# An attention and two matrix stages on one core: from slot 16 on three engines issue in a written order, with the second attention in smaller steps

## The chip, the core and the metric

The kernel runs on one core of a Trainium2 chip. PE multiplies matrices into PSUM (eight banks), ACT does functions and copies, DVE elementwise work and transposes, POOL further elementwise work, and SP issues DMAs. Each engine takes its own instructions in order and waits on semaphores for the others. The metric is the device time of one execution in microseconds. Before the change it is 1663.2 us, the median of three runs (1661.97 to 1664.64).

## The reference

```python
# q, k, v: 8 batches x 8 heads x 576 x 64; p: 8 x 8 x 32 x 64; all float32
p_packed = sm_attn(p, k, v)                    # 32 packed rows per head
out = sm_attn(q, p_packed, p_packed)           # second attention, 576 rows
x = out as tokens x 512                        # 4608 tokens
h = x @ moe_w_in; g = h * cos(h); x = g @ moe_w_out          # 512 -> 2048 -> 512
h = x @ moe2_w_in                                            # 512 -> 2048
P = a0 + a1*h + a2*h**2 + a3*h**3
Q = 1 + |b0|*|h| + |b1|*h**2
out = (P / (Q + 1e-6)) @ moe2_w_out
```

## The kernel before

The program has three parts. The first, up to some 120 us, makes the packed rows of every batch. The second part, which the change touches, has 128 slots, 16 for each of the 8 batches. It doesn't form the attention's output: the second attention gives only its weights (ah and al, a value and its rest, which together stand for one float32), and the packed rows are multiplied into w_in beforehand (W', tile wq, high and low part). The third part is the last matrix stage (L773 and L860).

A slot n covers 288 tokens (half a batch) and 256 of the 2048 hidden columns. `mm_h` has 12 matmuls of 288 columns (L580) that give h in PSUM. `chain1` makes g from it: u on ACT (L605), r on DVE (L606), the absolute value and the sine on ACT (L610, L611), g on DVE (L612). One slot later `finish_g` splits g into gh (ACT, L66) and gl (DVE, L67). `mm_y(n-2)` takes gh and gl two slots later: 24 matmuls (L634) that add to four PSUM banks y0 to y3. After the eight slots of a half each bank is copied as yh and yl (L66, L67) and stored (L656, L657). For batch 0 the half is done in two pieces, and a piece stored earlier, yp, is added first (L652).

h has two PSUM buffers, used in turn. The scores of the second attention (L192) take the next buffer of the same two. So the h that follows scores gets the buffer of the h just ahead of them, which is free once g has read it.

Beside this, while batch b runs, the following is done on ACT, DVE and POOL. `attn2_steps` is a generator that does the second attention of batch b+1 in steps: transposes of q (qT) and packed rows (ppb), scores and the maximum (sT), Exp on ACT (L376, with a table load ahead, and another one back to the sine), the sums (sm), scaling and transposing (aT), ah and al. `split_wq` splits a quarter of W' for the next batch: the high part on ACT (L66), the rest on DVE (L67); quarter j serves slots 2j, 2j+1, 2j+8 and 2j+9 of its batch. `conv_w2` turns every third slot a piece of the third part's weights into two words: cvf on DVE and POOL (L79, L84, L88), cvh on ACT (L92), cvl on POOL (L93), two stores.

The order of instructions on each engine is not that of the code. A scheduler chooses it at build time from the dependences and the free buffers, and `hold` only keeps an instruction behind another one. The order within PE's stream is therefore a mixture: pieces of y and of h of several slots alternate.

Of the kernel before, what the change touches and what calls it, by code (L numbers as in the profile page):

```python
# [20 lines left out]
def pack_attention_moe_moe_kernel(  # L21
# [90 lines left out]
    if True:  # L112
# [210 lines left out]
        def attn2_steps(b, pool, new_ps, tg, now):  # L323
            def load(g):
                t = pool.tile([128, C, D], F32, tag="qx", bufs=1, name="qx")
                nc.sync.dma_start(out=t, in_=q[b, 4 * g:4 * g + 4].rearrange("h (j c) d -> (h j) c d", c=C))
                return t

            def tile(shape, dt, nm):
                tag, bufs = tg.get(nm, (nm, 1))  # L330
                return pool.tile(shape, dt, tag=tag, bufs=bufs, name=nm)

            t = load(0)
            if b == 1:
                ppb_t[0] = pool.tile([128, NDB, 4, M], F32, name="ppb")
                nc.gpsimd.memset(ppb_t[0], 0.0)
            ppb = ppb_t[0]
            sT = pool.tile([128, G, C, M], F32, tag="sT", bufs=1, name="sT")
            yield
            for g in range(G):  # L340
                qT = tile([128, NDB, C, 32], F32, "qT")
                hold(
                    nc.vector.transpose(  # L343
                        out=qT.rearrange("p e c j -> p c e j"), in_=t.rearrange("p c (e i) -> p c e i", e=NDB)
                    ),
                    now(),
                )
                if b == 0:
                    ppT = tile([128, NDB, M], F32, "ppT")
                    hold(nc.vector.transpose(out=ppT.rearrange("p e m -> p (e m)"), in_=pp[:, b * G + g]), now())  # L350
                else:
                    ppT = ppb
                    for h in range(4):
                        r = slice(32 * h, 32 * h + 32)
                        hold(
                            nc.vector.transpose(
                                out=ppT[r, :, h], in_=pp[r, b * G + g].rearrange("p (e i) -> p e i", e=NDB)
                            ),
                            now(),
                        )  # L360
# [14 lines left out]
                yield  # L375
            nc.scalar.activation(out=sT, in_=sT, func=AF.Exp, scale=scale)  # L376
            sm = pool.tile([128, G, C], F32, tag="sm2", bufs=1, name="sm2")
            nc.vector.tensor_reduce(out=sm, in_=sT, op=ALU.add, axis=AX.X)
            nc.vector.tensor_scalar(out=sm, in0=sm, scalar1=1e-9, scalar2=None, op0=ALU.add)
            nc.vector.reciprocal(out=sm, in_=sm)  # L380
            yield
            for g in range(G):
                nc.vector.tensor_tensor(  # L383
                    out=sT[:, g], in0=sT[:, g], in1=sm[:, g].unsqueeze(2).to_broadcast([128, C, M]), op=ALU.mult
                )
                aT = tile([128, C, 32], F32, "aT")
                nc.vector.transpose(out=aT, in_=sT[:, g])
                ah = a_p[b % 2].tile([128, S], F32R, tag="ah", bufs=2, name="ah")
                al = a_p[b % 2].tile([128, S], F32R, tag="al", bufs=2, name="al")
                split(ah, al, aT.rearrange("p c j -> p (c j)"), nc.vector)  # L390
                a_t[b, g] = (ah, al)
                yield

        st_t = {}

# [62 lines left out]
        for i in range(at_ld0):  # L458
            cvs[i][0](cvs[i][2])

        tg0 = {"qT": ("kT", 2), "aT": ("E", 2)}
        at = attn2_steps(
            0, wk, lambda nm: ps0.tile([128, 2, 512], F32, tag="s1", bufs=2, name=nm), tg0, lambda: None
        )
# [1 line left out]
        prep(1)  # L466
        for n in range(NG + 2):
            if n >= 3:
                next(at, 1)
            if n + 1 < NG:  # L470
                s1(n + 1)
            if n + 3 < NG:
                load_k(n + 3)
            if n + 2 < NG:
                load_v(n + 2)
                prep(n + 2)
            if n < NG:
                et(n)
            if 1 <= n <= NG:
                pv(n - 1)  # L480
            if n >= 2:
                ppt(n - 2)
            if n % 2 and n <= 2 * EARLY:
                conv_next()
# [32 lines left out]
        def conv_w2(i):  # L517
            fp = words_in(st_t.pop(("w2", i)), cv_p, 512, last_h[0])
            hi = at_p.tile([128, 512], F32R, tag="cvh", bufs=1, name="cvh")
            lo = at_p.tile([128, 512], F32R, tag="cvl", bufs=1, name="cvl")  # L520
            words_out(fp, hi, lo)
            nc.sync.dma_start(out=w2d[0][i], in_=hi.bitcast(F32))
            nc.sync.dma_start(out=w2d[1][i], in_=lo.bitcast(F32))


        NB = NT // 512
# [92 lines left out]
        def mm_y(n):  # L619
# [21 lines left out]
            if last and j < NJ - 1:  # L641
                for d in range(NKD):
                    t = we_p.tile([128, 512], F32, tag="wev", bufs=WEV, name="part")
                    nc.scalar.activation(out=t[:, 0:HS], in_=y_t[d][:, 0:HS], func=AF.Copy)
                    nc.sync.dma_start(out=yp[:, d], in_=t[:, 0:HS])
            elif last:
                t0 = b * S + hf * HS
                for d in range(NKD):
                    src = y_t[d][:, 0:HS]
                    if halves:  # L650
                        src = yp_t[0][:, d]
                        nc.vector.tensor_tensor(out=src, in0=src, in1=y_t[d][:, 0:HS], op=ALU.add)  # L652
                    yh = (pools["a"] if "a" in pools else at_p).tile([128, HS], F32R, tag="yh", bufs=2, name="yh")
                    yl = (pools["a"] if "a" in pools else at_p).tile([128, HS], F32R, tag="yl", bufs=2, name="yl")
# [13 lines left out]
            return psh[h_n[0] % len(psh)].tile([128, 2, 512], F32, tag="h", bufs=1, name=nm)  # L668

        at = None  # L670

        def slot(n):
            nonlocal at
# [9 lines left out]
                fill(2)  # L683
            fill(2)
            i2, ph2 = divmod(n - 16, 3)
            if 0 <= i2 < 2 * NFC:
                if ph2 == 0:
                    load_w2(i2)
                elif ph2 == 2:
                    conv_w2(i2)  # L690
            if b + 1 < B:
                if s == (0 if b else LATE):
                    at = attn2_steps(b + 1, at_p, h_tile, {"aT": ("qT", 1)}, lambda: last_h[0])
                if s % 2 == 1 if b else s >= LATE:
                    next(at, 1)
                if s == 15:
                    for _ in at:
                        pass
                if b == 0 and s in (12, 13):
# [4 lines left out]
                for jj, (sl, ss) in enumerate(((2 if b else 8, 7 if b else 11), (10, 13), (12, 15), (14, 16))):  # L704
# [4 lines left out]
            if b > 0 and s == 0:  # L709
                split_wq(b, 3, nc.vector, last_h[0])  # L710
            move_in(n)

# [27 lines left out]
        for n in range(len(slots)):  # L740
            if n == LATE:
# [3 lines left out]
                psh.append(  # L745
                    ehp.enter_context(tc.tile_pool(name="pshb", bufs=1, space=PSUM, side="right", **RW))
                )
            slot(n)
# [4 lines left out]
        mm_y(len(slots) - 1)  # L753
        move_in(len(slots) + 1)
        e1k.close()
        ehp.close()
# [157 lines left out]
```

## Time and profile before

| | |
|---|---|
| time, median of 3 runs | 1663.2 us (1661.97 to 1664.64) |
| time of the profiled execution | 1665.62 us |
| its span | 1663.6 us |
| PE busy, share of the span | 1595.3 us, 96% |
| DVE busy | 1252.1 us, 75% |
| ACT busy | 1200.8 us, 72% |
| POOL busy | 158.2 us, 10% |
| mean granted clock of PE | 0.986 of full speed |

The span runs from the first to the last instruction. Matmuls overlap, so their listed durations are longer than their distance; the distance is read from a run of them (start to start). For the second part the waits of PE and the work of DVE and ACT between two h are what to look at.

### The profile page before, as it was taken

What the parts mean: (1) busy time and instruction counts of PE and PEld (TensorE: products, weight loads), DVE (VectorE), ACT (ScalarE), POOL (GpSimd) and SP (SyncE); (2) the same over time, 40 slices, a digit from 0 to 9 for tenths busy, and PEclk for the clock granted to TensorE, in tenths of its full rate; (3) what the DMA queues carried; (4) which work ended last, traced back from release to release, by engine and by line L of the source; (5) the groups of instructions that cost most, each with busy time, mean ns of one, the idle gap of its engine ahead of it and who ended that gap; (6) DMA issues with size and microseconds to landing.
All of it is one profiled execution on the core that took longest, in us unless ns stands there. A gap on an engine that the chain in (4) does not pass through costs nothing.

```text
span 1663.6 us, 25747 instructions
## 1 busy us (share of the span) xinstructions
PE 1595.3 (96%) x9792; PEld 1353.8 (81%) x9792; DVE 1252.1 (75%) x1934; ACT 1200.8 (72%) x1973; POOL 158.2 (10%) x120
## 2 busy tenths in 40 slices
PE   6789988999999999999999999999999999999997
PEld 3446668999999999999998888888888888888886
DVE  5745568777868777868558888888888888888886
ACT  3467657676768677768668877877777778787875
POOL 1014330112111112121000000000000000000000
PEclk9889999999999999999999999999999999999999
DMA  9957774344444444445292101010110202020010
GB/s 273 246 151 241 245 213 134 116 142 133 137 133 125 139 144 133 136 127 179 63 303 110 54 24 51 26 51 26 37 40 3 74 1 76 1 76 1 12 40 26
DMA packets 98427, 176.40 MB, mean 106 GB/s; under 512 B 11648, under 2 KB 42880, under 8 KB 98304
## 3 DMA queue, kind: packets, MB, share of 16 engines
q1 hardware_dynamic: 97984, 174.23, 34.4%
q8 instruction: 77, 1.26, 0.3%
q10 hardware_dynamic: 320, 0.52, 0.1%
q14 instruction: 46, 0.38, 0.1%
HBM read 114.36 MB, written 60.36 MB: 105 GB/s over the span
## 4 chain that ended last, share of the span: by engine, by line
PE 75%; DVE 8%; ACT 5%; issue 2%; DMA 2%; POOL 0%; SPq 0%; DVEq 0%; ACTq 0%; POOLq 0%
PE h L773 24%; PE o L860 24%; PE y L634 16%; PE h L580 8%; PE w L307 1%; PE s L192 1%; DVE r L606 1%; ACT r L610 1%; DVE g L612 1%; DVE gl L67 1%; ACT r L611 1%; PE w L284 1%; DVE wq L67 1%; DVE qT L343 1%; DVE sT L383 1%
## 5 line engine op out<-in xcount | busy, mean ns | idle before, releaser
L634 PE MATMUL y<-gh,w1o 128*128 128x288 f32 x2048 | 440.7, 301 | 4.1 <-ACT gh L66 2.6
L773 PE MATMUL h<-x,w 128*128 128x512 f32 x1728 | 422.2, 393 | 0.0
L773 PEld LDWEIGHTS h<-x,w 128*128 128x128 f32 x1728 | 324.2, 188 | 74.3
L634 PEld LDWEIGHTS y<-gh,w1o 128*128 128x128 f32 x2048 | 338.5, 190 | 17.0 <-issue 7.7
L860 PE MATMUL o<-w,g2h 128*128 128x512 f32 x1152 | 332.9, 393 | 1.2 <-ACT g2h L791 1.2
L634 PE MATMUL y<-gl,w1o 128*128 128x288 f32 x1024 | 300.6, 300 | 8.3 <-DVE gl L67 8.2
L860 PEld LDWEIGHTS o<-w,g2h 128*128 128x128 f32 x1152 | 216.2, 188 | 51.1 <-ACT g2h L791 2.1
L580 PE MATMUL h<-ah,wq 128*128 128x288 f32 x1024 | 231.8, 302 | 14.0 <-DVE g L612 13.2
L634 PEld LDWEIGHTS y<-gl,w1o 128*128 128x128 f32 x1024 | 194.6, 190 | 15.5 <-DVE gl L67 11.8
L860 PE MATMUL o<-w,g2l 128*128 128x512 f32 x576 | 199.9, 393 | 0.0
L806 ACT ACTIVATE sq<-h 128x512 f32<-128x512 f32 x144 | 87.6, 608 | 154.6 <-PE h L773 154.6
L580 PEld LDWEIGHTS h<-ah,wq 128*128 128x128 f32 x1024 | 173.1, 190 | 24.2 <-issue 19.2
L808 DVE SCALAR_TENSOR_TENSOR ab<-sq,coef,ab 128x512 f32<-128x512 f32 x144 | 108.2, 751 | 66.0 <-ACT ab L807 65.8
L612 DVE SCALAR_TENSOR_TENSOR g<-h,r 128x576 f32<-128x576 f32 x128 | 95.6, 753 | 79.6 <-ACT r L611 79.0
L580 PE MATMUL h<-al,wq 128*128 128x288 f32 x512 | 151.7, 296 | 0.0
L605 ACT ACTIVATE u<-h,coef 128x576 f32<-128x576 f32 x128 | 94.3, 739 | 74.0 <-PE h L580 73.5
L817 DVE SCALAR_TENSOR_TENSOR ab<-ab,y 128x512 f32<-128x512 f32 x144 | 99.5, 691 | 48.7 <-ACT y L814 48.7
L860 PEld LDWEIGHTS o<-w,g2l 128*128 128x128 f32 x576 | 108.2, 188 | 24.6
L606 DVE SCALAR_TENSOR_TENSOR r<-u,h 128x576 f32<-128x576 f32 x128 | 95.3, 748 | 38.6 <-ACT u L605 38.2
L67 DVE TENSOR_TENSOR gl<-g,gh 128x576 fp32r<-128x576 f32 x128 | 99.7, 780 | 30.4 <-ACT gh L66 28.5
L809 ACT ACTIVATE c<-h,coef 128x512 f32<-128x512 f32 x144 | 114.3, 794 | 8.5 <-DVE g2l L797 8.4
L66 ACT ACTIVATE gh<-g 128x576 fp32r<-128x576 f32 x128 | 87.3, 682 | 40.9 <-DVE g L612 38.2
(98 smaller groups left out, 2315.6 us busy)
## 6 DMA issues: line engine op xcount, KB each, us to landing
x<-yd SPq DMA_DIRECT2D x36, 512.0 KB
w<-w2d SPq DMA_DIRECT2D x68, 256.0 KB
st<-in_moe_w_in_dram SPq DMA_DIRECT2D x32, 512.0 KB
st<-in_moe_w_out_dram SPq DMA_DIRECT2D x32, 512.0 KB
wq<-wd SPq DMA_DIRECT2D x56, 256.0 KB
wd<-wev SPq DMA_DIRECT2D x48, 256.0 KB
kx<-in_k_dram SPq DMA_DIRECT2D x16, 576.0 KB
vx<-in_v_dram SPq DMA_DIRECT2D x48, 192.0 KB
```

The source lines that it names most:

```text
L67: lo_eng.tensor_tensor(out=lo, in0=src, in1=hi.bitcast(F32), op=ALU.subtract)
L580: last_h[0] = nc.tensor.matmul(out=ps[:, u, 0:HS], lhsT=wq[:, g, a, o:o + 128], rhs=a_t[b, g][c][:, hf * HS:hf * HS + HS], start=(i == 0), ...
L605: nc.scalar.activation(out=u, in_=ph, func=AF.Identity, bias=coef[:, 6:7])
L606: nc.vector.scalar_tensor_tensor(out=r, in0=u, scalar=RND, in1=ph, op0=ALU.subtract, op1=ALU.subtract)
L612: nc.vector.scalar_tensor_tensor(out=gt, in0=ph, scalar=2.0 * math.pi, in1=r, op0=ALU.mult, op1=ALU.mult)
L634: nc.tensor.matmul(out=y_t[d][:, 0:HS], lhsT=w1o_s[f // 4][a][:, f % 4, 128 * d:128 * d + 128], rhs=gs[c][:, u], start=(first and u == 0 a ...
L773: nc.tensor.matmul(out=ps, lhsT=w2_s[f][:, 0, a, 128 * kk:128 * kk + 128], rhs=x_t[t, c, kk], start=(i == 0), stop=(i == 3 * NKD - 1),)
L806: nc.scalar.activation(out=sq, in_=ph, func=AF.Square)
L808: nc.vector.scalar_tensor_tensor(out=ab, in0=sq, scalar=coef[:, 5:6], in1=ab, op0=ALU.mult, op1=ALU.add)
L809: nc.scalar.activation(out=c1, in_=ph, func=AF.Identity, scale=coef[:, 3:4], bias=coef[:, 2:3])
L817: nc.vector.scalar_tensor_tensor(out=ab, in0=ab, scalar=QC, in1=y0, op0=ALU.add, op1=ALU.mult)
L860: nc.tensor.matmul(out=o_t[s], lhsT=g2_t[n][a][:, 128 * s:128 * s + 128], rhs=w2_s[f][:, 1, c], start=(f == 0 and i == 0), stop=(f == NFC ...
```

## The change

From slot 16 to the end of the second part ACT, DVE and PE issue in the order of the code. The steps of the second attention are smaller (qT and ppb apart, Exp and sums apart, the last ones in another arrangement) and a table tells how many are done at the end of which slot. Three of the four splits of W' move: those of quarters 1 and 2 from slots 13 and 15 to slots 0 and 2 of the next batch, that of quarter 3 from slot 0 to slot 3, that of quarter 0 from slot 7 to 8. The second half of a weight piece (cvh, cvl, stores) comes a slot later. yh and yl have four buffers, in the last batch three and two. In the first second attention aT uses another buffer.

```diff
+                yield
                 if b == 0:
...
             nc.scalar.activation(out=sT, in_=sT, func=AF.Exp, scale=scale)
+            yield
...
+            turn(0)
+            yield
+            high(0)
+            turn(1)
+            yield
+            high(1)
+            low(0)
+            low(1)
+            yield
...
-        tg0 = {"qT": ("kT", 2), "aT": ("E", 2)}
+        tg0 = {"qT": ("kT", 2), "aT": ("kT", 2)}
...
+            def finish():
+                words_out(fp, hi, lo)
...
-                    yh = (pools["a"] if "a" in pools else at_p).tile([128, HS], F32R, tag="yh", bufs=2, name="yh")
+                    pool, bh, bl = (pools["a"], 3, 2) if "a" in pools else (at_p, 4, 4)
+                    yh = pool.tile([128, HS], F32R, tag="yh", bufs=bh, name="yh")
+                    yl = pool.tile([128, HS], F32R, tag="yl", bufs=bl, name="yl")
...
+        STEPS = {0: 1, 2: 1, 3: 1, 4: 1, 5: 1, 6: 1, 7: 1, 10: 1, 11: 1, 12: 1, 13: 1, 14: 1}
+        STEPS0 = {0: 1, 1: 2, 2: 3, 3: 3, 4: 2, 5: 1}
...
+                    ((2, 8), (10, 16), (12, 18), (14, 19)) if b else ((8, 11), (10, 13), (12, 15), (14, 16))
...
+            if b > 1 and s < 4:
+                for jj, ss in ((1, 0), (2, 2), (3, 3)):
+                    if s == ss:
+                        split_wq(b, jj, nc.vector)
...
+            if n == 16:
+                by_hand.enter_context(
+                    tc.manual_schedule(engines={mybir.EngineType.Activation, mybir.EngineType.DVE, mybir.EngineType.PE})
+                )
```

In batch 4, slots 66 and 67 (its slots 2 and 3), DVE had this order before, with the stores' parts yl of the half just ended between the work of the slots:

```order
L67 TENSOR_TENSOR yl<-y_5537,yh 128x288
L612 SCALAR_TENSOR_TENSOR g<-h,r 128x576
L67 TENSOR_TENSOR yl<-y_5538,yh 128x288
L343 STREAM_TRANSPOSE qT<-qx 128x18x2x32
L356 STREAM_TRANSPOSE ppb<-pp 32x2x32 x4
L606 SCALAR_TENSOR_TENSOR r<-u,h 128x576
L67 TENSOR_TENSOR gl<-g,gh 128x576
L67 TENSOR_TENSOR yl<-y_5539,yh 128x288
L606 SCALAR_TENSOR_TENSOR r<-u,h 128x576
```

Now DVE has, in the same two slots:

```order
L631 SCALAR_TENSOR_TENSOR r<-u,h 128x576
L67 TENSOR_TENSOR gl<-g,gh 128x576
L637 SCALAR_TENSOR_TENSOR g<-h,r 128x576
L79 TENSOR_SCALAR cvf<-st_5909 128x512
L84 SCALAR_TENSOR_TENSOR cvf<-st_5909,cvf 128x512
L343 STREAM_TRANSPOSE qT<-qx 128x18x2x32
L67 TENSOR_TENSOR wq<-wq 128x2x512
L631 SCALAR_TENSOR_TENSOR r<-u,h 128x576
L67 TENSOR_TENSOR gl<-g,gh 128x576
L637 SCALAR_TENSOR_TENSOR g<-h,r 128x576
L357 STREAM_TRANSPOSE ppb<-pp 32x2x32 x4
L67 TENSOR_TENSOR wq<-wq 128x2x512
```

Each slot is now r, gl, g and then the other work of the slot, to which a split of W' (wq) has moved in both.

On PE scores were put between pieces of y before (s is the scores' tile, y_7013 and the like are banks; the place is in batch 5):

```order
L634 MATMUL y_7014<-gh,w1o 128x288
L634 MATMUL y_7014<-gl,w1o 128x288
L634 MATMUL y_7014<-gh,w1o 128x288
L192 MATMUL s_7212<-qT,ppb 128x288 x4
L634 MATMUL y_7011<-gh,w1o 128x288
L634 MATMUL y_7011<-gl,w1o 128x288
```

They now stand between the end of a slot's y and the next h, here in slot 4 of batch 4:

```order
L659 MATMUL y_6017<-gh,w1o 128x288
L659 MATMUL y_6017<-gl,w1o 128x288
L659 MATMUL y_6017<-gh,w1o 128x288
L192 MATMUL s_6168<-qT,ppb 128x288 x4
L605 MATMUL h<-ah,wq 128x288
L605 MATMUL h<-al,wq 128x288
```

The h behind the scores is the one that takes the buffer of the h ahead of them.

In the last batch DVE's parts of the first half's banks, yl, had other work between them before:

```order
L67 TENSOR_TENSOR yl<-y_8486,yh 128x288
L67 TENSOR_TENSOR yl<-y_8487,yh 128x288
L612 SCALAR_TENSOR_TENSOR g<-h,r 128x576
L67 TENSOR_TENSOR yl<-y_8488,yh 128x288
L606 SCALAR_TENSOR_TENSOR r<-u,h 128x576
L67 TENSOR_TENSOR gl<-g,gh 128x576
L67 TENSOR_TENSOR yl<-y_8489,yh 128x288
```

At the same place they now stand together, behind g and ahead of the next slot's r:

```order
L637 SCALAR_TENSOR_TENSOR g<-h,r 128x576
L67 TENSOR_TENSOR yl<-y_8477,yh 128x288
L67 TENSOR_TENSOR yl<-y_8478,yh 128x288
L67 TENSOR_TENSOR yl<-y_8479,yh 128x288
L67 TENSOR_TENSOR yl<-y_8480,yh 128x288
L631 SCALAR_TENSOR_TENSOR r<-u,h 128x576
```

The next r, and with it everything on DVE, has moved behind all four.

## Rows read from the trace of the kernel before

**Rows 1.** Busy time by stretch: count in brackets, clock, DMA share, GB/s
```profile
264.00:854.00 590.00, 571.24 (x4156) 560.03 (x4154) 432.58 (x644) 418.19 (x631) 91.45 (x64) 0.99 0.45 138
854.00:1660.00 806.00, 800.97 (x3482) 651.65 (x3480) 664.10 (x1016) 632.09 (x1049) 0.00 (x0) 1.00 0.13 43
```

**Rows 2.** PE's waits, 264 to 854: us in total, times, longest
```profile
PE h L580 <- DVE g L612: 8.5, 9, 1.6
PE y L634 <- DVE gl L67: 7.5, 10, 2.0
PE y L634 <- ACT gh L66: 2.6, 1, 2.6
```

**Rows 3.** Chain of waits, 305 to 325: start, us, what
```profile
308.85 3.18 PE y L634 x24
...
321.58 1.94 PE s L192 x8
```

**Rows 4.** Chain of waits, 330 to 345
```profile
338.46 4.45 PE y L634 x20
```

**Rows 5.** Timeline of ACT, 795 to 799: start, us, ..., idle before and releaser
```profile
795.34 0.74 ACT L605 ACTIVATE u<-h,coef 128x576 f32<-128x576 f32 x1 [1.62 <-PE h L580]
...
797.63 0.78 ACT L611 ACTIVATE r<-r,coef 128x576 f32<-128x576 f32 x1
```

**Rows 6.** Timeline of DVE, 795 to 799
```profile
796.12 0.75 DVE L606 SCALAR_TENSOR_TENSOR r<-u,h 128x576 f32<-128x576 f32 x1 [1.61 <-ACT u L605]
798.44 0.76 DVE L612 SCALAR_TENSOR_TENSOR g<-h,r 128x576 f32<-128x576 f32 x1 [1.57 <-ACT r L611]
```

**Rows 7.** Groups by line, 284 to 854: busy us, mean ns | idle before
```profile
L67 DVE TENSOR_TENSOR wq<-wq 128x1024 fp32r<-128x1024 f32 x24 | 36.3, 1514 | 5.1 <-ACT wq L66 5.0
L67 DVE TENSOR_TENSOR yl<-y,yh 128x288 fp32r<-128x288 f32 x52 | 22.6, 452 | 13.4 <-ACT yh L66 10.4 <-DMA yd<-yl 2.8
L84 DVE SCALAR_TENSOR_TENSOR cvf<-st,cvf 128x512 uint32<-128x512 uint32 x31 | 21.3, 687 | 0.4
L343 DVE STREAM_TRANSPOSE qT<-qx 128x1152 f32<-128x1152 f32 x11 | 15.1, 1370 | 0.0
L79 DVE TENSOR_SCALAR cvf<-st 128x512 uint32<-128x512 uint32 x31 | 13.0, 419 | 0.0
L356 DVE STREAM_TRANSPOSE ppb<-pp 32x64 f32<-32x64 f32 x48 | 10.8, 225 | 0.6
L67 DVE TENSOR_TENSOR al<-aT,ah 128x576 fp32r<-128x576 f32 x12 | 10.4, 869 | 0.2
L387 DVE STREAM_TRANSPOSE aT<-sT 128x576 f32<-128x576 f32 x12 | 9.2, 768 | 0.0
L378 DVE TENSOR_REDUCE sm<-sT 128x36 f32<-128x1152 f32 x6 | 8.1, 1352 | 3.2 <-ACT sT L376 3.2
```

**Rows 8.** Timeline of DVE, 342 to 348
```profile
342.79 1.22 DVE L67 TENSOR_TENSOR wq<-wq 128x1024 fp32r<-128x1024 f32 x1
...
345.20 1.86 DVE L67 TENSOR_TENSOR gl<-g,gh 128x576 fp32r<-128x576 f32 x1
```

**Rows 9.** Timeline of POOL, 344 to 348
```profile
344.75 1.70 POOL L88 TENSOR_TENSOR cvf<-cvf,st 128x512 uint32<-128x512 uint32 x1 [8.95 <-DVE cvf L84]
```

**Rows 10.** Timeline of ACT, 256 to 260
```profile
256.82 1.28 ACT L376 ACT_TABLE_LOAD   x1
258.11 1.17 ACT L376 ACTIVATE sT<-sT 128x1152 f32<-128x1152 f32 x1
```

**Rows 11.** Timeline of DVE, 783 to 787
```profile
783.63 0.82 DVE L67 TENSOR_TENSOR yl<-y,yh 128x288 fp32r<-128x288 f32 x2 [1.05 <-ACT yh L66]
...
786.51 0.46 DVE L67 TENSOR_TENSOR yl<-y,yh 128x288 fp32r<-128x288 f32 x1 [1.15 <-DMA yd<-yl]
```

**Rows 12.** Timeline of DVE, 262 to 267
```profile
264.93 0.76 DVE L612 SCALAR_TENSOR_TENSOR g<-h,r 128x576 f32<-128x576 f32 x1 [0.61 <-ACT r L611]
```

**Rows 13.** Timeline of PE, 262 to 290
```profile
266.90 1.16 PE L634 MATMUL y<-gh,w1o 128*128 128x288 f32 x4 [2.60 <-ACT gh L66]
```

More of the change, by code (lines that the diff above doesn't have):

```diff
@@ L381, in attn2_steps, with turn @@
             yield
-            for g in range(G):
+            aT = tile([128, G, C, 32], F32, "aT")
+            def turn(g):
                 nc.vector.tensor_tensor(
@@ L385, in attn2_steps, with high, low @@
                 )
-                aT = tile([128, C, 32], F32, "aT")
-                nc.vector.transpose(out=aT, in_=sT[:, g])
+                nc.vector.transpose(out=aT[:, g], in_=sT[:, g])
+            def high(g):
                 ah = a_p[b % 2].tile([128, S], F32R, tag="ah", bufs=2, name="ah")
                 al = a_p[b % 2].tile([128, S], F32R, tag="al", bufs=2, name="al")
-                split(ah, al, aT.rearrange("p c j -> p (c j)"), nc.vector)
+                nc.scalar.activation(out=ah, in_=aT[:, g].rearrange("p c j -> p (c j)"), func=AF.Copy)
                 a_t[b, g] = (ah, al)
-                yield
+            def low(g):
+                ah, al = a_t[b, g]
+                nc.vector.tensor_tensor(
+                    out=al, in0=aT[:, g].rearrange("p c j -> p (c j)"), in1=ah.bitcast(F32), op=ALU.subtract
+                )
[8 more added lines that the diff above has]
+            yield
         st_t = {}
@@ L468, in pack_attention_moe_moe_kernel @@
             if n >= 3:
-                next(at, 1)
+                for _ in range(2 if n in (4, 6, 8) else 1):
+                    next(at, 1)
             if n + 1 < NG:
@@ L520, in conv_w2 @@
             lo = at_p.tile([128, 512], F32R, tag="cvl", bufs=1, name="cvl")
-            words_out(fp, hi, lo)
-            nc.sync.dma_start(out=w2d[0][i], in_=hi.bitcast(F32))
-            nc.sync.dma_start(out=w2d[1][i], in_=lo.bitcast(F32))
+            def finish():
+                words_out(fp, hi, lo)
+                nc.sync.dma_start(out=w2d[0][i], in_=hi.bitcast(F32))
+                nc.sync.dma_start(out=w2d[1][i], in_=lo.bitcast(F32))
+            return finish
         NB = NT // 512
@@ L652, in mm_y @@
                         nc.vector.tensor_tensor(out=src, in0=src, in1=y_t[d][:, 0:HS], op=ALU.add)
-                    yh = (pools["a"] if "a" in pools else at_p).tile([128, HS], F32R, tag="yh", bufs=2, name="yh")
-                    yl = (pools["a"] if "a" in pools else at_p).tile([128, HS], F32R, tag="yl", bufs=2, name="yl")
+                    pool, bh, bl = (pools["a"], 3, 2) if "a" in pools else (at_p, 4, 4)
+                    yh = pool.tile([128, HS], F32R, tag="yh", bufs=bh, name="yh")
+                    yl = pool.tile([128, HS], F32R, tag="yl", bufs=bl, name="yl")
                     split(yh, yl, src, nc.vector)
@@ L670, in pack_attention_moe_moe_kernel @@
         at = None
+        w2_out = []
+        STEPS = {0: 1, 2: 1, 3: 1, 4: 1, 5: 1, 6: 1, 7: 1, 10: 1, 11: 1, 12: 1, 13: 1, 14: 1}
+        STEPS0 = {0: 1, 1: 2, 2: 3, 3: 3, 4: 2, 5: 1}
+        by_hand = ExitStack()
         def slot(n):
@@ L685, in slot @@
             i2, ph2 = divmod(n - 16, 3)
+            if 0 <= i2 <= 2 * NFC and ph2 == 0 and w2_out:
+                w2_out.pop()()
             if 0 <= i2 < 2 * NFC:
@@ L689, in slot @@
                 elif ph2 == 2:
-                    conv_w2(i2)
+                    w2_out.append(conv_w2(i2))
             if b + 1 < B:
@@ L693, in slot @@
                     at = attn2_steps(b + 1, at_p, h_tile, {"aT": ("qT", 1)}, lambda: last_h[0])
[L694 to L699, printed above, removed]
+                for _ in range(STEPS.get(s, 0) if b else STEPS0.get(s - LATE, 0)):
                     next(at, 1)
@@ L703, in slot @@
                     nc.sync.dma_start(out=yp_t[0], in_=yp)
-                for jj, (sl, ss) in enumerate(((2 if b else 8, 7 if b else 11), (10, 13), (12, 15), (14, 16))):
+                for jj, (sl, ss) in enumerate(
+                    ((2, 8), (10, 16), (12, 18), (14, 19)) if b else ((8, 11), (10, 13), (12, 15), (14, 16))
+                ):
                     if s == sl:
@@ L708, in slot @@
                         split_wq(b + 1, jj, nc.vector, last_h[0])
-            if b > 0 and s == 0:
+            if b > 1 and s < 4:
+                for jj, ss in ((1, 0), (2, 2), (3, 3)):
+                    if s == ss:
+                        split_wq(b, jj, nc.vector)
+            if b == 1 and s == 0:
                 split_wq(b, 3, nc.vector, last_h[0])
@@ L747, in pack_attention_moe_moe_kernel @@
                 )
+            if n == 16:
+                by_hand.enter_context(
+                    tc.manual_schedule(engines={mybir.EngineType.Activation, mybir.EngineType.DVE, mybir.EngineType.PE})
+                )
             slot(n)
@@ L753, in pack_attention_moe_moe_kernel @@
         mm_y(len(slots) - 1)
+        by_hand.close()
         move_in(len(slots) + 1)
```

## The prediction

> **What bounds the kernel now.** I read the busy time by stretches first. From 854 us on, the third matrix stage keeps PE busy for 801 of 806 us [rows 1]; nothing of the change lies there, so it only moves as a block. From 264 to 854 us, where the change lies, PE is busy for 571 of 590 us, while DVE has 433 us of work and ACT 418 [rows 1]. PE is the bound, and what can be won is its waits. The list of PE's waits for that stretch has 20 entries in three pairs: 8.5 us for g (the PSUM buffer of h is not free), 7.5 us for gl, 2.6 us once for gh [rows 2], 18.6 us in all. The chain of waits shows the steady pace: 24 matmuls of y in 3.18 us, 8 score passes in 1.94 us [rows 3]. So one matmul takes 0.1325 us, a slot (12 of h, 24 of y) 1.59 + 3.18 = 4.77 us. After its longest wait but one (2.0 us, [rows 2]) PE took 4.45 us for 20 matmuls of y [rows 4] where 20 x 0.1325 = 2.65 is the pace: 1.8 us more, at a granted clock below full speed. Something like it follows the 2.6 us wait. I put before's loss that the change can touch at 18.6 + about 3.5 = 22 us.
>
> **The slot as a clock.** All the rest is worked from one undisturbed slot, near the end of the stage. Call the start of u(n) zero: ACT u at 795.34, Sin at 797.63 [rows 5], DVE r at 796.12, g at 798.44 [rows 6]. So r starts at 0.78, g at 3.10 and ends at 3.86. Instructions queued back to back start some 0.08 us before the listed end of the one ahead (two yl of 0.45 take 0.82, [rows 11]), so DVE is free at 3.78 and ACT at 3.00. The next u starts at 4.77, the next r at 5.55. DVE therefore has 5.55 - 3.78 = 1.77 us a slot for other work, ACT as much; more makes the next r late by the excess, and the lateness L carries on. PE starts y(n-1) at 4.57. It takes gl(n-1) as second matmul, which ends at 0.78 + 0.67 + 0.75 = 2.2 + L: PE waits once L is over 2.4. After a score matmul the next h goes into the PSUM buffer of the h just before, so it needs g's end (3.86 + L) at 4.57 - 1.59 + 1.94 = 4.92: PE waits once L is over 1.0.
>
> **The change part by part.** From slot 16 on the three engines issue as written: PE h(n), y(n-2), h(n+1), ..., DVE r, gl, g and then the slot's other work. Until 264 us PE's order is row for row the old one; the moved pieces of the first second attention lie on DVE between transposes that wait for loads there, and I cost them at 0 (between -1 and +1; without that cover they would show as up to two of its 0.75 us pieces).
> The other work, with the 0.08 taken off [rows 7]: a split of W' 1.44 (1.22 less the overlap, 1.15, where nothing shares the port [rows 8]), yl 0.37 each, the two cvf of a W2 piece 0.34 + 0.61 = 0.95, qT 1.29, ppb 4 x 0.23 = 0.9, aT 0.69, al 0.79 and the scaling ahead of aT like al. W2 pieces come every third slot, so batches 1 and 4, 2 and 5, 3 and 6 are alike.
> Port: gl took 1.86 us in place of 0.75 while POOL ran cvf's sum, and ended 0.61 us after it [rows 8, 9]. In the written order ACT, free from 3.00, first does cvh; the POOL step that waits for it then starts at about the time, 3.78, at which a split, a scaling or an al wants to. Each such meeting costs up to 1.1 us; I carry both none and all.
>
> (A) *The h after the first score matmul (slot 5 of batches 2 to 6).* Three splits now stand in slots 0, 2 and 3. Batch 4: slot 2 has 0.95 + 1.29 + 1.44 = 3.68, so L = 1.91; slot 3 has 0.9 + 1.44, so L = 2.48; less 1.0 that is a wait of 1.5. The others come to 1.4 and 1.5. Five of them: 7.4 us; with splits of 1.15, 4.5.
> (B) *The exponential (slots 10 to 14, batches 1 to 6).* Table load and Exp take 1.29 + 1.08 on ACT [rows 10]: free at 3.00 + 2.37 = 5.37, so u(11) is 0.6 late; the load back to Sin adds 1.29: g(11) is 1.9 late. The sums behind it (1.27 + about 0.5) eat the free 1.77, so L = 1.9, plus 0.95 in batches 1 and 4. Slots 12 to 14 bring 1.5, 1.5 and 1.6 for 1.77 free, so L never drains while W2 pieces come on top. Waits on gl, and of the next batch's first h on al: 0.4 to 2.5 a batch; 2.4 us in all without port meetings, 9.7 with all.
> (C) *Between two halves (slots 1 and 9).* y of the next half takes bank d after yl(d). The last, yl(3), ends at 3.78 + 3 x 0.38 + 0.46 = 5.37; PE wants it at 4.57 + 9 x 0.1325 = 5.76. The margin is 0.35, and the split of slot 0 follows an L from (B) of 0.5 to 1.4. Waits: 1.8 us in all at the least, 6.5 at the most. The four buffers take away the wait of yh and yl for stores in batches 1 to 6; that wait now sat beside PE work and is worth nothing by itself.
> (D) *The last batch.* There yl has two buffers still. In the trace yl(2) started 2.88 us after yl(0), held by the store [rows 11], and the old order had g between and PE had h to do. As written PE stands at bank 2: 3.78 + 2.88 + 0.46 = 7.12 against 4.57 + 0.8. That is 1.75 us twice, 3.5 (to 5 with some L).
> (E) *The start (slots 16 to 18).* The first h needs al of batch 1. DVE's order is g, aT, aT, g, gl, al, al from 264.93 [rows 12]: al(0) ends at 264.93 + 0.67 + 1.38 + 0.67 + 0.67 + 0.75 = 269.07. PE is free at 266.90 - 2.60 = 264.30 [rows 13], so it waits 4.8 us; y, which it did here, now stands behind. In slot 17 each sum of yp waits behind the yl ahead, which waits for its yh, 1.3 us a bank: the fourth is 2.4 late. 7.2 in all. This replaces 2.60 [rows 13], the longest wait on g, 1.6, and one of the shorter ones on gl [rows 2].
>
> Sum of the new waits, low and high: A 4.5 to 7.4, B 2.4 to 9.7, C 1.8 to 6.5, D 3.5 to 5, E 7.2: 19.4 to 35.8. The terms hang on port meetings that go either way, so I take the middle, 27.6. Slow clock after waits: before 3.5; now one long wait and some of 1.5 to 1.8, taken as the same (0 to 5 more). Difference 27.6 - 18.6 = +9.0. The profiled execution took 1665.62 us (span 1663.6), so 1674.6 by it; it is 2.4 over the median of 1663.2, and by the median I predict **1672 us**.
>
> A rule that would make it worse: the Trainium skill, page "ScalarE: Activation LUTs", section "What ACT_TABLE_LOAD costs", gives a load 1.28 us and a drain of 1.38 behind it. Here Exp started 1.29 after its load [rows 10], so the trace has the first and not the second. By the page, (B) would have L = 4.7 and wait 2.3 more in each of six batches, an estimate of 1686; by the row the sum stands.
>
> **The rivals.** (1) *All meetings at the port at full price, with the clock following.* For it: order and length of the instructions repeat, so a meeting that happens once happens in each like batch. Against: where DVE starts first, POOL waits, at no cost. 35.8 - 18.6 + 3 = +20: 1683. Chance 0.20. (2) *No meeting.* 19.4 - 18.6 = +1: 1664, no change. Chance 0.13. (3) *The slack of two slots swallows every lateness*, so A, B and C are nothing and only D and E stay: 10.7 - 18.6 = -8: 1655, faster. It decides at L below 1.0 in slot 4 and below 2.4 in slots 12 to 15. For it: DVE's 433 us of 590 leave room on average. Against: the batch's work stands in a few slots. Chance 0.10. (4) *The engines don't follow the written order*; the printed order speaks against it. Chance 0.02, no change.
>
> **How the numbers follow.** My forecast has 0.55: waits between 23 and 33 us, 1667 to 1678. The range takes in half of rival 1 and most of rival 2: 1661 to 1683. A change within 0.2% (3.3 us) can't be told from none here. Slower: 0.55 + 0.20 + a little of rival 2, 0.77; same 0.13; faster 0.10.
>
> **What would show it.** PE's waits for g at six or more places right after a score matmul (A) and for gl one to three slots after the Exp (B); a wait of about 5 us ahead of slot 16's h (E); two waits of about 2 us in the last batch on yl (D); PE's waits in this stage 25 to 35 us in place of 18.6. I am wrong if they are below 15, or if PE's clock is lower over whole batches.

## The result and the profile after

The changed kernel takes 1675.4 us (median of 5 runs, 1671.5 to 1679.3) against 1663.2 before: ratio 1.007, 95% interval 1.0043 to 1.0096. It is slower by 12 us; 1672 was predicted. The profiled execution took 1675.36 us, its span is 1673.6, 10.0 more than before.

Busy time by stretch, columns as in [rows 1]. The third stage comes later and takes as long as it did; the loss is in the second part:

```profile
264.00:854.00 590.00, 564.05 (x4083) 548.66 (x4082) 429.97 (x638) 410.14 (x624) 89.38 (x64) 1.00 0.42 133
864.00:1670.00 806.00, 801.06 (x3480) 651.46 (x3478) 664.51 (x1016) 630.83 (x1049) 0.00 (x0) 1.00 0.13 44
```

In 806 us of the third stage PE is busy for 801, before and after. In the 590 us from 264 us on PE is busy for 7.2 us less than in [rows 1], at a granted clock no lower. So the answer lies in PE's waits: the list of them from 264 us to the last matmul of y (us in total, times, longest):

```profile
PE y L659 <- DVE yl L67: 7.1, 8, 1.7
PE h L605 <- DVE g L637: 5.5, 5, 1.4
PE y L659 <- DVE gl L67: 5.0, 10, 0.6
PE h L605 <- ACT ah L395: 3.2, 1, 3.2
PE h L605 <- DVE al L400: 3.1, 3, 1.2
PE y L659 <- DVE yp L677: 1.8, 3, 0.7
```

25.7 us in 30 waits, where [rows 2] has 18.6 in 20. The list counts idle time from the modelled end of the matmul ahead. Counted from start to start, less the pace of 0.1325, the 30 gaps of more than 0.3 us are 31.2 us in all; the 20 of before are 21.9. The difference is 9.3 us of the 10.3 by which the stretch from the first of these waits to the last y has grown (595.8 us before, 606.1 now). The other 1.0 us is a balance: smaller gaps add some 2.5 us, and one slow stretch of the clock less (below) takes some 1.5 away. Before's three pairs have become six, and each has its place:

*The start (E).* PE's timeline, with the idle time and its releaser in brackets: the first h of batch 1 waits for ah, then for al, where [rows 13] has y in front.

```profile
267.60 0.40 PE L605 MATMUL h<-ah,wq 128*128 128x288 f32 x1 [3.17 <-ACT ah L395]
269.18 0.40 PE L605 MATMUL h<-al,wq 128*128 128x288 f32 x1 [1.18 <-DVE al L400]
```

*Behind scores (A).* DVE's timeline in slots 2 to 4 of batch 2: the splits of quarters 2 and 3, and the g that they make late.

```profile
374.76 1.18 DVE L67 TENSOR_TENSOR wq<-wq 128x1024 fp32r<-128x1024 f32 x1
...
379.85 1.23 DVE L67 TENSOR_TENSOR wq<-wq 128x1024 fp32r<-128x1024 f32 x1
...
383.30 0.76 DVE L637 SCALAR_TENSOR_TENSOR g<-h,r 128x576 f32<-128x576 f32 x1 [0.89 <-ACT r L636]
```

PE then starts the next h 0.15 us after that g ends:

```profile
384.21 0.37 PE L605 MATMUL h<-ah,wq 128*128 128x288 f32 x1 [0.82 <-DVE g L637]
```

It comes five times, once in each of batches 2 to 6. DVE stands idle for 0.89 us just ahead of this g: it waits for the sine with the next work already queued behind g. That gap comes slot after slot, 99.8 us in 110 slots (DVE's group of g, columns as in [rows 7]), and the experiments use it.

```profile
L637 DVE SCALAR_TENSOR_TENSOR g<-h,r 128x576 f32<-128x576 f32 x110 | 83.4, 758 | 99.8 <-ACT r L636 99.8
```

*The exponential (B).* ACT's timeline in slots 10 and 11 of batch 1, with both table loads:

```profile
330.37 1.28 ACT L377 ACT_TABLE_LOAD   x1
331.66 1.17 ACT L377 ACTIVATE sT<-sT 128x1152 f32<-128x1152 f32 x1
...
334.99 1.28 ACT L636 ACT_TABLE_LOAD   x1
```

Two slots later POOL and DVE meet, in POOL's timeline and in DVE's:

```profile
343.55 1.30 POOL L93 TENSOR_TENSOR cvl<-cvf,cvh 128x512 fp32r<-128x512 f32 x1 [3.20 <-ACT cvh L92]
```

```profile
343.66 1.81 DVE L387 TENSOR_TENSOR sT<-sT,sm 128x576 f32<-128x576 f32 x1
```

The scaling, 0.75 us alone, began 0.11 us after POOL and ended 0.62 us after POOL had done. In the next slot PE waits 0.4 us for gl. The ten waits for gl lie in slots 12 to 14 of batches 1, 3, 4 and 6.

*Ends of halves (C).* Six waits for yl, 0.2 to 1.2 us, one at the first y of each of batches 2 to 7; at the second halves of batches 1 to 6 there is none.

*The last batch (D).* DVE's timeline at the end of its first half, then PE's:

```profile
790.92 0.81 DVE L67 TENSOR_TENSOR yl<-y,yh 128x288 fp32r<-128x288 f32 x2
793.51 0.88 DVE L67 TENSOR_TENSOR yl<-y,yh 128x288 fp32r<-128x288 f32 x2 [1.77 <-DMA yd<-yl]
```

```profile
794.02 0.40 PE L659 MATMUL y<-gh,w1o 128*128 128x288 f32 x1 [1.53 <-DVE yl L67]
```

The third yl starts 2.59 us after the first, held by a store as in [rows 11], and bank 2 is what PE waits for.

The clock went the other way. Before had two stretches of 3.4 us at half speed (1.2 GHz) in this part, after has one; each began during or just after a wait of PE. The one that followed before's 2.0 us wait is gone (windows, before and then after; the clock is the third number from the end):

```profile
334.00:350.00 16.00, 13.91 (x91) 13.71 (x92) 14.52 (x19) 12.15 (x20) 4.37 (x3) 0.89 0.37 116
```

```profile
334.00:350.00 16.00, 15.04 (x112) 14.57 (x110) 11.85 (x18) 10.75 (x17) 2.61 (x2) 1.00 0.55 159
```

### The profile page after: what moved, and what is told of

The parts are those of the page before. It is cut to its first block, busy times and chain, and to the rows that moved or that the text cites. A ratio compares the mean times of both kernels' runs of the same rounds, so it can differ in the third digit from the quotient of the medians.

```text
span 1673.6 us, 25700 instructions
## 1 busy us (share of the span) xinstructions
PE 1598.3 (96%) x9792; PEld 1353.7 (81%) x9792; DVE 1251.9 (75%) x1934; ACT 1196.4 (71%) x1973; POOL 156.1 (9%) x120
## 4 chain that ended last, share of the span: by engine, by line
PE 67%; DVE 12%; ACT 11%; DMA 5%; issue 3%; SPq 1%; DVEq 0%; ACTq 0%
PE h L811 24%; PE o L898 23%; PE y L659 10%; PE h L605 5%; ACT r L635 3%; ACT r L636 3%; DVE r L631 3%; PE w L307 1%; DVE wq L67 1%; DVE g L637 1%; DMA vx<-in_v_dram 1%; DMA kx<-in_k_dram 1%; DMA st<-in_moe_w_in_dram 1%; PE s L192 1%; DVE sT L387 1%
## 5 line engine op out<-in xcount | busy, mean ns | idle before, releaser
L659 PE MATMUL y<-gl,w1o 128*128 128x288 f32 x1024 | 305.0, 299 | 5.9 <-DVE gl L67 5.6
L635 ACT ACTIVATE r<-r 128x576 f32<-128x576 f32 x128 | 87.8, 687 | 97.3 <-DVE r L631 97.2
L847 ACT ACTIVATE c<-h,coef 128x512 f32<-128x512 f32 x144 | 114.0, 792 | 8.2 <-DVE g2l L835 8.2
L848 ACT ACTIVATE c<-h,coef 128x512 f32<-128x512 f32 x144 | 114.7, 797 | 0.0
```

The costliest lines, as they stand in the source:

```text
L635: nc.scalar.activation(out=r, in_=r, func=AF.Abs)
L659: nc.tensor.matmul(out=y_t[d][:, 0:HS], lhsT=w1o_s[f // 4][a][:, f % 4, 128 * d:128 * d + 128], rhs=gs[c][:, u], start=(first and u == 0 a ...
L847: nc.scalar.activation(out=c1, in_=ph, func=AF.Identity, scale=coef[:, 3:4], bias=coef[:, 2:3])
L848: nc.scalar.activation(out=c0, in_=ph, func=AF.Identity, scale=coef[:, 1:2], bias=coef[:, 0:1])
```

## The experiments

Times are medians; a ratio is to the kernel before on the same chip, with its 95% interval. "Stage" runs from the start of PE's wait at the first slots of batch 1 to the last y. In the traces of the runs it starts between 257 and 267 us, so single executions differ by some us for what lies ahead of it, and the length of the stage is given where that matters. The theory at the start: the written order costs, as the other work of a slot stands behind g and ahead of the next r.

**1. The order taken away.**

```diff
-            if n == 16:
-                by_hand.enter_context(tc.manual_schedule(engines={...}))
```

> The changed kernel without its written order: the scheduler chooses again, all else of the change stays (small steps, moved splits, four buffers). Theory (the written order costs, because lateness made by a slot's other work now stands ahead of the next r and PE has nothing else to do): PE's waits from 264 us to the last y fall from 25.7 us back to 14 to 22, ratio to the kernel before 0.997 to 1.003. Rival (the new places of steps and splits cost, in whatever order): waits stay at 24 or more, above all those for g behind scores, ratio 1.005 to 1.010.

1682.5 us, ratio 1.011 (1.0078 to 1.0142). It is no faster than with the order (1.007, 1.0043 to 1.0096), so the theory in this form falls; the waits, 32.9 us in all and more for g than for anything else, are the rival's. The three largest groups of PE's waits in the stage:

```profile
PE h L605 <- DVE g L637: 14.5, 10, 2.9
PE y L659 <- DVE yl L67: 6.4, 8, 1.3
PE y L659 <- ACT gh L66: 6.2, 4, 2.6
```

One of 2.5 us, at 323.55, has a chain behind it that ACT's timeline shows: the second half of a weight piece was put ahead of the next u, and waited 2.29 us for POOL.

```profile
318.69 0.63 ACT L92 ACTIVATE cvh<-cvf 128x512 fp32r<-128x512 f32 x1 [2.29 <-POOL cvf L88]
```

So the new layout alone costs some 20 us, and the written order gives some 7 of them back, though the intervals of the two ratios overlap. The other waits of this run I did not trace to their causes.

**2. The layout taken away.** The kernel before with the written order alone.

```diff
+            if n == 16:
+                by_hand.enter_context(tc.manual_schedule(engines={...}))
             slot(n)
```

> The kernel before, with only the written order added from slot 16 on; its steps of the second attention and its splits stay where they were. Theory (order and layout belong together: the layout with large steps puts scalings, transposes, parts and a split in one slot's end, 4 us and more for 1.77 free, and PE pays the excess nearly every odd slot): PE's waits from 264 us on are over 70 us, 1710 us or more. Rival (the written order as such costs some 10 us, the layout is of no matter for it): 1665 to 1685.

1788.3 us (one run). The stage is 723 us, 127 more than before. PE's largest groups of waits, 100 us in all with the rest:

```profile
PE h L580 <- ACT ah L66: 29.4, 8, 6.8
PE y L634 <- DVE yl L67: 22.1, 13, 3.4
PE y L634 <- DVE gl L67: 17.1, 19, 1.7
```

Start to start the gaps are 93 us more than before. The rest goes with the clock: it is at half speed for 99 us of the stage (6.8 before), in stretches behind such waits.

Either part alone is worse than both. The change is one thing in two halves, and its 12 us are what is left of the order's price after the layout has taken 113 us off it.

**3. Lateness moved.**

```diff
-                    ((2, 8), (10, 16), (12, 18), (14, 19)) if b else ((8, 11), (10, 13), (12, 15), (14, 16))
+                    ((2, 8), (10, 15), (12, 18), (14, 19)) if b else ((8, 11), (10, 13), (12, 15), (14, 16))
...
-                for jj, ss in ((1, 0), (2, 2), (3, 3)):
+                for jj, ss in ((3, 0), (2, 2)):
```

> Quarter 1's split back into slot 15 of the batch ahead, quarter 3's from slot 3 to slot 0; slot 3 is left without one. Theory (lateness adds up over slots 2 and 3, PE waits behind the scores of slot 4 once it is over 1.0): slot 3 ends with 1.91 + 0.9 - 1.77 = 1.0, so the five waits for g behind scores (5.5 us) fall to under 0.2 each; the split in slot 15 adds at most 0.5 us at a few ends of batches. 4 to 6 us less than the changed kernel, about 1670, ratio 1.003 to 1.005. Rival (the three DVE passes on the scores of slot 4 make g late, not the splits): the five waits stay at 0.8 to 1.5 us and the time stays at 1675.

1678.1 us, ratio 1.0088 (1.0057 to 1.0118). The mechanism was right and the time was not: there is no wait for g any more, but all waits together are 27.6 us in place of 25.7:

```profile
PE y L659 <- DVE yl L67: 14.1, 8, 2.0
PE y L659 <- DVE gl L67: 5.6, 14, 0.6
```

yl has gone from 7.1 to 14.1. The splits of slots 15 and 0 leave lateness to slot 1, and there the four yl stand in front of PE's next bank. The stage is 6.7 us longer than the changed kernel's, and most of that is the clock. Behind three of these waits of about 2 us it fell to half speed, here after the one that ended at 450.8:

```profile
448.00:458.00 10.00, 8.06 (x50) 7.84 (x49) 7.97 (x12) 7.42 (x13) 1.85 (x2) 0.83 0.57 183
```

**4. A later start.**

```diff
-            if n == 16:
+            if n == 18:
```

> The written order starts with slot 18 in place of 16. Theory: h of slot 16 waits for ah and al (3.2 + 1.2 us) only because y, which could run there, is written behind it; with the old order there, the 7.1 us lost between 264 and 286 us become 3 to 5, as before; 2 to 4 us less than the changed kernel, ratio 1.004 to 1.006. Rival (ah and al come late whatever the order, and the wait is only moved into y): the stretch costs the same within 1 us, ratio 1.007.

1669.9 us, ratio 1.0049 (1.0024 to 1.0073), 5.5 less than the changed kernel. The two intervals overlap; the stage, 602.7 us, is 3.4 less, as expected. The waits for ah, al and yp at the start are replaced by a short one for gl and by one for gh, as the kernel before has it:

```profile
PE y L659 <- ACT gh L66: 2.6, 1, 2.6
```

**5. y bank by bank at the ends of halves.** The loops that follow go by this list.

```diff
+            order = [(u, d) for u in range(2) for d in range(NKD)]
+            if n >= 16 and (first or last):
+                order.sort(key=lambda t: t[1])
...
```

> In the slots that begin and end a half (from slot 16 on) the 24 matmuls of y go bank by bank (6 for a bank) instead of twice round the four banks. The computation is the same. Theory (PE stands at banks whose yl comes late: terms C and D): bank 3 is wanted 18 matmuls after bank 0 instead of 9, 1.2 us later, bank 2 0.8 later, and bank 0 is ready for its copy 1.2 us earlier; PE's 7.1 us for yl fall to 1.5 to 3, about 5 us less than the changed kernel, near 1670. Rival (lateness of DVE from the other work sets the end, and PE pays it at the next gl or g): the waits for yl fall but those for g and gl rise as much, 1675.

1670.1 us, ratio 1.0048 (1.003 to 1.0066), 5.3 less, with an interval that overlaps that of the changed kernel. The trace, of an execution that took 1674.6, bears out only a part of it: yl goes from 7.1 to

```profile
PE y L661 <- DVE yl L67: 5.7, 8, 1.1
```

and yp from 1.8 to 0.5, but g and gl are no lower. In the last batch the two waits are down from 1.5 and 1.7 to 0.9 and 1.0. At the other ends of halves PE still waits as long as before, at its first bank: there the lateness is in the first yl, which no order of banks helps. All waits together are 23.6 us in place of 25.7, a gain of some 2 us, and the interval of the ratio allows that. Term D was not taken away by itself: with four buffers each for the last batch's yh and yl, the pool that follows would need 37 KB per partition where 34.3 are left.

**6. No table loads.** The exponential of the second attention of batches 2 to 7 is left out; a copy stands in its place.

```diff
-            nc.scalar.activation(out=sT, in_=sT, func=AF.Exp, scale=scale)
+            nc.scalar.activation(out=sT, in_=sT, func=AF.Copy, scale=scale)
```

> The exponential of the second attention is left out from batch 2 on (a copy stands in its place, which needs no other table), so the two table loads of a batch go. Theory (term B: the loads make g of slot 11 1.9 us late and the batch's last steps never drain it): PE's waits for gl (5.0) and for al of batches 2 and 5 (2.2 of the 3.1) fall to 1 or less together, those for yl by 1 to 3; 8 to 10 us less than the changed kernel in the profiled run. Rival (the port meetings of scaling, al and gl with POOL make the lateness, the loads only start it): gl and al fall by less than half.

1660.0 us (one run), 15 less; the stage, 594.3 us, is 11.8 less, which is more than was expected. All ten waits for gl are gone, and of al's the two between batches fell from 1.0 us to 0.5 each:

```profile
PE y L659 <- DVE yl L67: 5.6, 6, 2.0
PE h L605 <- DVE g L637: 5.5, 5, 1.4
```

The meetings at the port are still there: the scaling takes 1099 ns in the mean and al 1110, as in the changed kernel (1102 and 1111). Without the loads they make PE wait for no gl: the loads make the lateness, and the meetings only add to it. The waits for g behind scores are the same to 0.1 us, so A and B are separate, as the prediction had them.

**7. The idle 0.9 us filled, first try.** `mids` holds pieces of DVE's other work, each put in some slots ahead; one of them is now done between gl and g. The rest of the edit, which fills `mids`, is left out here.

```diff
             finish_g(n - 1)
+            if mids:
+                mids.pop(0)()
             nc.scalar.activation(out=r, in_=r, func=AF.Abs)
```

> DVE's other work goes partly between gl and g of a slot, where DVE stood idle 0.9 us for the sine in every slot: the two cvf of a weight piece, ppb, the two al, and the splits of quarters 2 and 3 in halves; the second half of a weight piece comes one slot later again. Theory (PE waits because the written order puts all of it behind g, ahead of the next r): 0.9 us of each slot is won back, so the waits for g behind scores (5.5) go, gl and al (5.0 + 2.2) fall to 2 or less, yl to 4: 10 to 14 us less than the changed kernel, 1661 to 1666. Rival (the piece of 0.95 between gl and g makes g and the whole chain late, and POOL's sum then meets another DVE instruction): 1672 to 1680.

1674.9 us, ratio 1.0081 (1.0058 to 1.0104): no gain, and the rival's number. The waits for g went and gl fell to 2.2, but yl rose to 9.1 and new ones came:

```profile
PE h L631 <- DVE al L400: 6.9, 7, 1.3
PE h L631 <- DVE wq L535: 3.0, 2, 1.5
PE s L192 <- DVE ppb L357: 1.7, 3, 0.8
```

Three kinds of piece (al of the second half of heads, the last half of a split, ppb) stood in the very slot in which PE wants them.

**8. Start, ends of halves and first fill together** (the edits of 4, 5 and 7).

> Written order from slot 18, y bank by bank at the ends of halves, and DVE's other work between gl and g, together. Theory: the gains add, as they lie in different places: 3 to 5 + 3 to 5 + 8 to 12 us less than the changed kernel, 1654 to 1661, at or below the kernel before. Rival (one lateness pays for the other, so the second remedy finds nothing left): not below 1662.

1669.9 us, ratio 1.0052 (1.0031 to 1.0074). The waits of the fill stayed (al 5.8, wq 3.0, ppb 1.8 us), so the rival's number came, for the reason of run 7.

**9. The fill with each piece a slot ahead of its use.** The later start and the banks of runs 4 and 5 are in it, and in the last batch yh and yl share five buffers. A part of the edit is shown.

```diff
-        STEPS = {0: 1, 2: 1, 3: 1, 4: 1, ...}
+        STEPS = {0: 1, 2: 1, 4: 1, 5: 1, 7: 1, 10: 1, 11: 1, 12: 1, 13: 1, 14: 1}
+        MIDS = (3, 6, 12, 13, 14)
...
+            for jj, sa, parts in ((1, 14, ((0, 15, 1), (1, 16, 1))), (2, 15, ((0, 17, 1), (1, 18, 1))), (3, 18, ((0, 19, 0), (1, 20, 1)))):
```

> The refill done again, each piece a slot earlier than it is wanted: between gl and g stand ppb (slots 3, 6), the two scalings (12, 13), al of the first half of heads (14), the cvf, and the splits of quarters 1 and 2 in halves (15, 16 and 17, 18); quarter 3's halves stand behind g in slots 3 and 4 (the latter between gl and g); written order from slot 18, y bank by bank at the ends of halves, and the last batch's yh and yl share five buffers. Theory (lateness that is made in a slot and not drained by the end of the next is what PE pays; the first refill failed because ppb, al and the halves of quarter 3 stood in the slot that wants them): PE's waits for al, wq, ppb and g behind scores go (17 us of the first refill), 8 to 15 us stay in all; 1645 to 1657, faster than the kernel before. Rival (POOL's sums, which now start inside the slot, block what follows on DVE, and the lateness comes back as waits for gl and yl): 1662 to 1672.

1645.1 us, ratio 0.9903 (0.9878 to 0.9929): faster than both kernels, 16 us below the one before by the ratio and 18 by the medians. The stage is 582.6 us, 13 below the kernel before and 23.5 below the changed one. PE waits 2.6 us for gh at its start, as in run 4, and five times after that:

```profile
PE y L709 <- DVE yl L67: 5.4, 4, 2.6
PE y L709 <- DVE gl L67: 0.7, 1, 0.7
```

The longest, 2.6 us for yl, is in the last batch: with five buffers the wait for a store is still there in its first half, and gone from its second.

DVE's timeline in slot 13 of batch 1 shows the fill: the scaling stands between gl and g, and g waits 0.16 us for the sine instead of 0.9.

```profile
334.15 0.81 DVE L67 TENSOR_TENSOR gl<-g,gh 128x576 fp32r<-128x576 f32 x1
334.89 0.75 DVE L387 TENSOR_TENSOR sT<-sT,sm 128x576 f32<-128x576 f32 x1
335.79 0.76 DVE L683 SCALAR_TENSOR_TENSOR g<-h,r 128x576 f32<-128x576 f32 x1 [0.16 <-ACT r L682]
```

**10. That fill alone**, without the later start, the banks and the shared buffers of the last batch.

> The changed kernel with the refill of the run before alone: written order from slot 16, y round the four banks as changed, the last batch's yh and yl with three and two buffers. Theory (the refill is what pays; start and ends of halves give their 4 to 6 us each beside it): 1645 + 4 to 6 (start) + 3 to 6 (ends of halves and last batch): 1652 to 1658; no wait for g behind scores or for gl after slot 18. Rival (the refill pays only with the ends of halves bank by bank, because lateness then goes over into the next half): 1662 or more.

1658.0 us, ratio 0.9967 (0.9945 to 0.9989), 17 less than the changed kernel and at the upper end of what was expected. The stage is 592.9 us, 13 less. What is left lies where the parts that were taken out act: ah, al and yp at the start (6.0 us together), and

```profile
PE y L707 <- DVE yl L67: 8.9, 5, 4.2
```

of which the longest is in the last batch. The fill is worth more than the other three parts together: 17 to 11 us by the ratios, 13 to 10 by the stage.

**11. Four buffers in the kernel before.**

```diff
-                    yh = (...).tile([128, HS], F32R, tag="yh", bufs=2, name="yh")
+                    yh = (...).tile([128, HS], F32R, tag="yh", bufs=2 if "a" in pools else 4, name="yh")
```

(yl likewise.)

> The kernel before, with only four buffers for yh and yl up to the last batch. Theory (as predicted: the wait for the stores stood beside PE's work and is worth nothing): ratio 0.998 to 1.002. Rival (yl that waits for a store holds DVE, and what stands behind it, so the buffers alone give the scheduled kernel 4 to 9 us): ratio 0.995 to 0.998.

1656.8 us, ratio 0.9965 (0.9949 to 0.9981): the rival. PE's waits from 262 us on are 15.1 us. With one of 0.7 us for gl at 261.4, which [rows 2] leaves out, before has 19.3; those for gl are 2.9 instead of 8.2:

```profile
PE h L580 <- DVE g L612: 9.6, 9, 2.3
PE y L634 <- DVE gl L67: 2.9, 5, 1.3
PE y L634 <- ACT gh L66: 2.6, 1, 2.6
```

ACT's yh waits 2.1 us for stores in place of 13.2, DVE's yl 1.1 in place of 2.8. Of the 4.2 us that PE waits less, 2.0 lie in slots 2 and 3, just behind the stores. The rest lies further on, and as the scheduler orders anew when a buffer is free earlier, the run shows what the buffers are worth and not the whole way by which.

**12. Two buffers in the changed kernel.**

```diff
-                    pool, bh, bl = (pools["a"], 3, 2) if "a" in pools else (at_p, 4, 4)
+                    pool, bh, bl = (pools["a"], 3, 2) if "a" in pools else (at_p, 2, 2)
```

> The changed kernel with two buffers for yh and yl in place of four. Theory (in the written order a yl that waits for a store holds DVE ahead of the next r, and PE stands at bank 2 as it does in the last batch, 1.7 to 1.9 us twice): the 11 ends of halves from batch 1 on (two each, the last batch's apart) lose 2 us and more each, with the lateness behind it: 1700 or more. Rival (as predicted, worth nothing by itself): within 3 us of 1675.

1710.0 us, ratio 1.0267 (1.024 to 1.0293):

```profile
PE y L659 <- DVE yl L67: 29.2, 21, 4.0
```

ACT's yh waits 25.6 us for stores (3.8 in the changed kernel) and DVE's yl 14.8 (1.8). In the written order that is a wait of PE at the ends of halves, as term D had it for the last batch. All waits are 43.4 us, 18 more than in the changed kernel; about as much again goes with the clock, at half speed for 41 us of the stage (3.4 there).

## Why the prediction was right, and where it was not

**The bound.** PE's waits were the right thing to count: 9.3 of 10.3 us of growth are gaps of PE, and 9.0 was the predicted difference. That the two are so near is in part luck. By the list in which the prediction had before's waits, the new ones are 25.7 us and the difference is 7.1. Start to start both sides are longer than the sum had them, 31.2 for 27.6 and 21.9 for 18.6, and these two errors cancel. Of the 3.4 us by which the time was missed most are the 2.4 taken off because before's profiled execution lay that much above its median; the changed kernel's lies at its median.

**The slot as a clock.** 1.77 us of free time a slot, 1.0 us to the wait behind scores and 2.4 to the one for gl, from one slot, placed the new waits of A and B in the slots where they came; those of C came at the ends of batches alone, where the prediction had slot 9 too. Run 3 confirms it for A (without a split in slot 3 all five waits go), run 6 for B. What it left out is the 0.9 us between gl and g. In this written order that time is lost, and filling it gave more than anything else that was tried (run 10).

**The terms**, predicted between both ends, against the list of waits:

| | predicted | measured |
|---|---|---|
| A, g behind scores | 4.5 to 7.4 | 5.5 |
| B, gl, and al of the next batch | 2.4 to 9.7 | 5.0 + 1.9 |
| C, ends of halves | 1.8 to 6.5 | 3.8 (7.1 less D) |
| D, last batch | 3.5 to 5 | 3.3 |
| E, start | 7.2 | 3.2 + 1.2 + 1.8 |
| sum | 27.6 taken | 25.7 |

A lies between its ends: the two splits took 1.18 and 1.23 us in slots 2 and 3 of batch 2, as the 1.22 of [rows 8] and less than the mean of [rows 7]. By such splits alone the sum had 4.5, so the wait itself was sized a little low. D and E were sized a little high: the store held yl for 2.59 us and not 2.88.

**The port.** The middle between no meeting and all was near, but it was chosen and not worked out. DVE's groups of the changed kernel by line, columns as in [rows 7]:

```profile
L67 DVE TENSOR_TENSOR gl<-g,gh 128x576 fp32r<-128x576 f32 x111 | 89.4, 805 | 0.9 <-ACT gh L66 0.8
L67 DVE TENSOR_TENSOR wq<-wq 128x1024 fp32r<-128x1024 f32 x24 | 31.1, 1297 | 4.2 <-ACT wq L66 4.0
L387 DVE TENSOR_TENSOR sT<-sT,sm 128x576 f32<-128x576 f32 x12 | 13.2, 1102 | 0.0
L400 DVE TENSOR_TENSOR al<-aT,ah 128x576 fp32r<-128x576 f32 x12 | 12.8, 1111 | 0.0
```

Alone, gl, scaling and al take 0.75 us and a split 1.22. Mean less that, times the count: 6.1, 1.8, 4.2 and 4.3, some 16 us of DVE in the stage. How much of it PE pays is not measured: no run takes the meetings alone away, and in run 6 they are there without a wait for gl. In run 9 the groups are

```profile
L67 DVE TENSOR_TENSOR gl<-g,gh 128x576 fp32r<-128x576 f32 x109 | 83.4, 765 | 0.8 <-ACT gh L66 0.8
L553 DVE TENSOR_TENSOR wq<-wq 128x512 fp32r<-128x512 f32 x36 | 33.8, 939 | 0.0
L387 DVE TENSOR_TENSOR sT<-sT,sm 128x576 f32<-128x576 f32 x12 | 9.0, 750 | 0.0
```

There the half splits pay (0.69 alone), mostly where nobody waits for them, and gl and the scaling don't. The Trainium skill, page "SBUF — State Buffer", section "Who interferes with whom", says that DVE and GpSimd share one port pair as an exclusive lock, held for a whole instruction. The scaling that began 0.11 us after POOL's cvl and ended 0.62 us after it agrees with it.

**The table load.** The drain that the Trainium skill, page "ScalarE: Activation LUTs", section "What ACT_TABLE_LOAD costs", gives behind a load is not seen in the trace after either: Exp starts 1.29 us after its load, and so does the sine. The estimate of 1686 that followed from it did not come.

**The slow clock** was taken as unchanged. In the profiled execution it was one stretch better than before, some 1.5 us, and no run shows that this had to be so. A wait of 2.6 us in run 8 is followed by no slow stretch, one of 1.4 us in run 12 is, and the same 3.2 us for ah at the start are followed by 3.4 us at half speed in the changed kernel and by 6.8 in run 3. Run 3 also shows the other side: three more stretches behind waits of 1.5 to 2 us.

**A step that was wrong.** "That wait now sat beside PE work and is worth nothing by itself", on the four buffers. In the kernel before they are worth 6 us (run 11), in the changed one 35 (run 12). The waits of ACT and DVE for the stores did stand beside PE's work, but the work behind them in the same streams was left out. Waits for gl in slots 2 and 3 show it with 2.0 us in the kernel before; how the rest of the 6 comes about is open. The sum was not touched by this, since C was worked out with four buffers in place.

**Rivals.** The slack of two slots did not swallow the lateness, and the engines do follow the written order. That the order as such is what costs, which I believed when the experiments began, is wrong too: with the old layout it costs 125 us (run 2), with the new one it costs nothing that run 1 can show, and rather gains some 7.

## What to carry to other kernels

An order written by hand repeats per slot, so work out the free time of each engine in one undisturbed slot, add up what each slot puts into it, and carry the excess on: where it passes the margin of the next thing that PE wants, PE waits. Put the other work into the gaps inside the chain, and a slot ahead of its use, before moving it from slot to slot; moving lateness alone only changes the place at which it is paid. A wait of an engine that isn't the bound can cost what stands behind it in its stream; in the fixed order here the same two buffers cost 35 us, in the scheduled one 6.

## What the runs showed that I had not expected

A piece of 0.95 us between gl and g, where 0.9 is free, did no harm: in run 9 the cvf stand there in 22 of the 32 slots that have them, and PE's wait for gl is 0.7 us in the whole stage. And two steps that are each slower, the layout (1682) and the order (1788), make a kernel of 1675 together. With the work placed otherwise, a later start, y bank by bank at the ends of halves and shared buffers in the last batch it is one of 1645.
